# Attention and a mixture of experts on one core: the first expert's eight weight splits set 4 and 5 steps apart

## The chip, the core and the metric

The kernel runs on one core of a Trainium2 chip. A core has a matrix engine (PE, with its weight loads listed as PEld), a vector engine (DVE), a scalar engine (ACT), a general engine (POOL) and a sync engine (SP), which here only issues DMAs. Each runs its own instructions in the order in which they stand, and waits on semaphores for the others. The metric is the device time of one execution in microseconds.

## The reference: attention, then each token through one of eight experts

```python
# attention: q, k, v are (8, 8, 576, 64): batch, heads, sequence, head size
scores = (1 / np.sqrt(64)) * np.matmul(q, k.transpose(0, 1, 3, 2))
thresh = np.max(scores, axis=-1, keepdims=True) - tau
scores = np.where(scores >= thresh, scores, -1000000000.0)
scores = scores - np.max(scores, axis=-1, keepdims=True)
attn = np.exp(scores)
attn = attn / (np.sum(attn, axis=-1, keepdims=True) + 1e-09)
out = np.matmul(attn, v)
x = out.transpose(0, 2, 1, 3).reshape(4608, 512)
# experts: w_gate (512, 8), w1 (8, 512, 1024), w2 (8, 1024, 512)
logits = x @ w_gate
expert_idx = np.argmax(logits, axis=1)
probs = softmax(logits)                       # with 1e-09 in the denominator
gate_w = probs[np.arange(N), expert_idx]
for e in range(8):
    mask = expert_idx == e
    h = np.maximum(x[mask] @ w1[e], 0.0)
    out[mask] = gate_w[mask, None] * (h @ w2[e])
```

## The kernel before

**Arithmetic.** Every fp32 operand of a product is split into two fp16 tiles: a high part (the scaled value rounded) and a low part (what the rounding left). A product is then three fp16 matmuls. A weight split is `split_w`: one ACT instruction rounds a loaded piece `wf` (128 partitions by 1024) into the high half of `wb` (L817). For the first expert, and for it alone, the low part is made in two halves by `low_part`: PE copies the rounded half into PSUM with a matmul against the identity (`hi_w`, L254), and DVE subtracts it from the scaled weight (L255). The other experts' low parts are one DVE instruction each (L825).

**Attention.** The 64 heads are 32 pairs, numbered 0 to 31. A pair has 11 steps of scores `s` (for the row maxima, `nm`, on DVE) and 11 steps of transposed scores `st`. For each `st` tile ACT makes exponentials `e` (L423), DVE multiplies them with the threshold mask (L426), ACT rounds two tiles at a time into `ph` (L431) and POOL makes the low part `pl` (L432; for two tiles of the last pair DVE does it). PE then multiplies `ph` and `pl` with the values `vop` into `av` (L476). ACT copies `av` out (L486, L491). When a batch of four pairs is done, `finish` divides by the sums (`xn`, L537), splits the rows into `R` (L544 on ACT, L545 on POOL, or on DVE for the last batch), SP transposes them by DMA into `xTg` (L552), and PE makes the logits `lg` (L570). `route` and `ranks` find each token's expert and place; POOL sends the rows out to `xs` (L644), once ACT has written the gate weights into `R` (L637).

**Experts.** `fetch` gathers a block of 128 tokens of one expert from `xs` (into `Rm` or `spare`, L858) and transposes it (`xTm`, or within `spare`, L868). `gemm1` makes `h` (L913), `gemm2` makes `y` (L946). Blocks 0 to 3 belong to the first expert. Some of `gemm1` of block 0 stands among the last steps of attention.

**Order.** The program is written step by step: a step `k` holds one `st` and one `s` tile, and `plan` and `after` hang other work on a step, ahead of it, in the middle of it (MID) or behind it (END). Step 0 is the first `st` step of pair 0, and KEND = 352 is one past the last of pair 31. The `s` tiles of pair 31 are steps 320 to 330. From step 336 on expert work is mixed in, 0.15 pieces a step, and from 352 on a piece a step. A scheduler then lays out each engine's queue from this, so rows can change places against the written order. The first expert's work hangs at `k` = 312:

```python
for i in range(8):
    plan(k + WS0 + WSD * i, lambda i=i: split_w(*wseq[i]))          # WS0 = 6, WSD = 2
    if i + 2 < 8:
        plan(k + WS0 + WSD * i, lambda i=i: load_w(*wseq[i + 2]))
```

The first two loads are asked for at step 313 (`room`). There are two `wf` buffers, so the load of piece i + 2 can start when piece i's low part has been made. Loads, transposes and the three row DMAs of each pair (`CQ<-ptT`, L394) all stand in SP's one queue.

Of the kernel before, what the change touches and what calls it, by code (L numbers as in the profile page):

```python
# [39 lines left out]
SW = 64.0  # L40
# [10 lines left out]
def kernel(  # L51
# [119 lines left out]
    FRONT, MID, END = range(3)  # L171
# [3 lines left out]
    def plan(k, f, where=END):  # L175
        if urgent[0]:
            f = hurry(f)
        assert (k, where) >= (now[0], slot[0])
        acts.setdefault(k, ([], [], []))[where].append(f)

    def hurry(f):

        def g():
            was, urgent[0] = urgent[0], True
            with tc.high_priority():
                f()
            urgent[0] = was

        return g

    def after(k, f, where=END):
        plan(now[0] + k, f, where)
# [55 lines left out]
    def low_part(x, hi, lo, scale, nm):  # L248

        sc = ps_sc.tile([P, 512], F32, tag="sc", name=f"hi_{nm}")  # L250
        y = sc[:, 0:hi.shape[1]] if len(hi.shape) == 2 else (
            sc[:, 0:hi.shape[1] * hi.shape[2]].rearrange("p (t d) -> p t d", t=hi.shape[1])
        )
        nc.tensor.matmul(y, ident_h, hi, start=True, stop=True)  # L254
        nc.vector.scalar_tensor_tensor(lo, x, scale, y, ALU.mult, ALU.subtract)  # L255
# [541 lines left out]
    def load_w(e, w, c):  # L797

        i = int(e != 0)
        wq[e, w, c] = wf = pools[i].tile([P, F], F32, tag="wf", name=f"wf_{e}_{c}_{w}", bufs=2 + 6 * i)  # L800
        if e in range(E):
            load = nc.sync.dma_start(wf, w12[e, :, c, w])
            if e == 1:
                tc.keep_in_program_order(load)
            return
        if e not in regs:
            regs[e] = nc.sync.value_load(T["esi"][0:1, e - E:e - E + 1], min_val=0, max_val=E - 1)
        nc.sync.dma_start(wf, w12[ds(regs[e], 1), :, c, w].rearrange("o p f -> (o p) f"))
# [3 lines left out]
    def split_w(e, w, c):  # L812
        wf = wq.pop((e, w, c))

        o = (wb1, wb2)[w][0 if e == "x" else e % 2][:, c].rearrange("p (a h d) -> p a h d", a=w + 1, h=2)
        x = wf.rearrange("p (a d) -> p a d", a=w + 1)
        hi = nc.scalar.activation(o[:, :, 0], x, AF.Copy, scale=SW)  # L817
        if e == 0:
            tc.keep_in_program_order(hi)
            for i in range(2):  # L820
                t = slice(512 * i, 512 * i + 512)
                y = (x[:, i], o[:, i, 0], o[:, i, 1]) if w else (x[:, 0, t], o[:, 0, 0, t], o[:, 0, 1, t])
                after(2, lambda y=y, i=i: low_part(*y, SW, f"w{w}_{c}_{i}"), END if i else MID)
            return
        nc.vector.scalar_tensor_tensor(o[:, :, 1], x, SW, o[:, :, 0], ALU.mult, ALU.subtract)  # L825

# [58 lines left out]
    def chunks(g):  # L885

        return 8 * shape(g)[1] // P
# [105 lines left out]
    WS0, WSD = TUNE["ws0"], TUNE["wsd"]  # L993
# [9 lines left out]
    for n in range(NPAIR):  # L1003

        k = NSTEP * (n - 1) - LEAD - SL
# [5 lines left out]
    for g in range(NG):  # L1011
        k = 2 * NSTEP * g
# [80 lines left out]
    wseq = [(0, w, c) for w in range(2) for c in range(4)]  # L1093
    k = NSTEP * (NPAIR - 2) - LEAD - SL
    plan(k + 1, room)
    for i in range(8):
        plan(k + WS0 + WSD * i, lambda i=i: split_w(*wseq[i]))
        if i + 2 < 8:
            plan(k + WS0 + WSD * i, lambda i=i: load_w(*wseq[i + 2]))
    TABLES = {B - 3: tables0, B - 2: tables1, B - 1: tables2}  # L1100
    plan(KEND + 12, close)

# [10 lines left out]
    k = 0  # L1113
# [3 lines left out]
    for i, g in enumerate(groups):  # L1117
        for j, m in enumerate(g):
            if m >= NF + 2:
                k = max(at[i - 2] + TUNE["fa"] if i >= 8 else 0, at[i - 3] + chunks(groups[i - 3]) + 1)  # L1120
# [10 lines left out]
    for e in range(1, E + NL):  # L1131
        for w in range(2):
            for c in range(4):
                i = 4 * w + c
                if e == 1:
                    k = 64 + TUNE["w1a"] + TUNE["w1b"] * i
                elif e < E:
                    k = 64 * e + (TUNE["wa1"], TUNE["wa2"])[w] + 7 * i
                else:
                    k = 16 * NEARLY + 16 * PL // P * (e - E) + (TUNE["wl1"], TUNE["wl2"])[w] + 2 * c  # L1140
# [22 lines left out]
    def weights(j):  # L1163
        turn[0] = j + 1
        split_done.add(wseq[j])
        split_w(*wseq[j])
        if j + 8 < len(wseq):
            k, e = when[j][:2]
            moe(
                max(chunk[0] + 1, k - (14 if e == 2 else 24)) if e < E else chunk[0] + 1,  # L1170
                lambda: asked[0] == j, lambda: (asked.__setitem__(0, j + 1), load_w(*wseq[j + 8])),
            )
# [4 lines left out]
    if True:  # L1177
# [15 lines left out]
        k = first  # L1193
# [45 lines left out]
    with tc.For_i(NL, total) as m:  # L1239
        idx = small.tile([P, 2], I32, tag="idx", name="idx_x", bufs=1)  # L1240
        nc.vector.tensor_copy(idx.unsqueeze(1), T["row"][:, ds(m, 1)])
        bad = small.tile([P, 2], I32, tag="badx", name="bad_x", bufs=1)
        nc.vector.tensor_copy(bad.unsqueeze(1), T["bad"][:, ds(m, 1)])
        regs["x"] = nc.sync.value_load(T["esi"][0:1, ds(m, 1)], min_val=0, max_val=E - 1)
        for w in range(2):
            for c in range(4):
                load_w("x", w, c)
                split_w("x", w, c)
        slots["x"] = idx, bad, 0
        fetch("x")  # L1250
        for g in gemm1, gemm2:
            for _ in g(("x",)):
                chunk[0] += 1
            while mo:
                for _, f in mo.pop(min(mo)):
                    f()
# [52 lines left out]
```

## Time and profile before

| what | value |
|---|---|
| median of 3 runs | 975.57 us (975.03, 975.57, 981.8) |
| the profiled execution | 974.36 us, span 972.6 us |
| mean granted clock of TensorE | 0.993 |
| busy in the span | PE 932.8, DVE 696.2, ACT 652.7, POOL 559.0 us |
| instructions | 28577 |

The span runs from the first to the last instruction; the profiled execution is 1.76 us longer than its span. Busy time is an average over stages. The attention part fills the span to about 570 us, the experts the rest, and the change lies between 505 and 600 us.

### The profile page before, as it was taken

The numbers are of one execution on the slowest core, as the hardware profiler recorded it, in microseconds if no ns is written. First come the engines' busy times: TensorE is split into PE (matmuls) and PEld (weight loads), VectorE is DVE, ScalarE is ACT, GpSimd is POOL, SyncE is SP. The second block draws the span as 40 slices with busy tenths as digits, with TensorE's granted clock in tenths as the row PEclk, the third lists the DMA queues.
The fourth block names the chain that finished last, engine by engine and source line by source line (L and its number), as shares of the span: only waits on it lengthen the run. The fifth ranks groups of instructions, "written<-read, shape, count | busy, mean of one in ns | idle before, by whom it ended". The sixth has DMA issues, their size and how long they took to land. (4 is left out here: it accounts for less than half of the span.)

```text
span 972.6 us, 28577 instructions
## 1 busy us (share of the span) xinstructions
PE 932.8 (96%) x11548; PEld 604.0 (62%) x11548; DVE 696.2 (72%) x1413; ACT 652.7 (67%) x1111; POOL 559.0 (57%) x467
## 2 busy tenths in 40 slices
PE   7899999999999999999997989999999999999997
PEld 2355555556556556565664677776677666677684
DVE  8899999999989999999999756835243341432650
ACT  2789898998988998989889944435333342433651
POOL 6466887897977998869979851531221212221121
PEclk9899999999999999999999999999999999999999
DMA  7642555474654674654647569998475565656720
GB/s 202 185 135 73 142 137 143 93 196 123 130 161 134 162 147 134 176 146 104 154 133 207 95 168 304 396 234 212 127 231 157 166 177 155 206 143 209 219 103 28
DMA packets 142707, 159.19 MB, mean 164 GB/s; under 512 B 96361, under 2 KB 112747, under 8 KB 142572
## 3 DMA queue, kind: packets, MB, share of 16 engines
q1 hardware_dynamic: 125782, 100.03, 41.1%
q10 hardware_dynamic: 7638, 27.85, 9.2%
q0 software_dynamic: 9152, 29.45, 8.9%
q8 instruction: 92, 1.51, 0.7%
q14 instruction: 43, 0.35, 0.1%
HBM read 90.24 MB, written 19.44 MB: 113 GB/s over the span
## 5 line engine op out<-in xcount | busy, mean ns | idle before, releaser
L432 POOL TENSOR_TENSOR pl<-e,ph 128x1024 f16<-128x1024 f32 x158 | 335.8, 2136 | 90.0 <-ACT ph L431 50.8
L423 ACT ACTIVATE e<-st,ntau 128x512 f32<-128x512 f32 (+1 forms) x352 | 222.2, 651 | 49.0 <-PE st L407 34.8
L426 DVE SCALAR_TENSOR_TENSOR e<-st,e 128x512 f32<-128x512 f32 (+1 forms) x352 | 219.1, 635 | 8.4 <-ACT e L423 7.8
L913 PEld LDWEIGHTS <-wb 128*128 128x128 f16 x2304 | 189.4, 98 | 20.3 <-DMA xTm<-Rm 1.3
L946 PE MATMUL y<-wb,hl 128*128 128x512 f16 (+1 forms) x1056 | 201.6, 360 | 0.0
L370 DVE TENSOR_REDUCE nm<-s 128x1 f32<-128x512 f32 x300 | 188.2, 631 | 14.7 <-PE s L360 13.4
L913 PE MATMUL h<-xTm,wb 128*128 128x256 f16 (+2 forms) x2112 | 196.3, 254 | 0.9 <-DVE lg L609 0.9
L476 PE MATMUL av<-vop,ph 128*128 128x65 f16 (+3 forms) x3072 | 187.7, 195 | 2.0 <-ACT x L486 1.2
L476 PEld LDWEIGHTS <-ph 128*128 128x128 f16 (+1 forms) x3072 | 157.8, 100 | 46.5 <-issue 17.0
L431 ACT CAST ph<-e 128x1024 f16<-128x1024 f32 x160 | 166.5, 1041 | 5.1 <-DVE e L426 4.5
L476 PE MATMUL av<-vop,pl 128*128 128x65 f16 (+1 forms) x1536 | 167.1, 194 | 2.1 <-POOL pl L432 1.6
L476 PEld LDWEIGHTS <-pl 128*128 128x128 f16 (+1 forms) x1536 | 135.7, 100 | 33.5 <-issue 9.8
L946 PEld LDWEIGHTS <-hl 128*128 128x128 f16 (+1 forms) x1056 | 94.1, 100 | 97.8 <-issue 1.9
L407 PE MATMUL st<-CQ,ck 128*128 128x512 f16 (+3 forms) x640 | 136.4, 287 | 4.6 <-DMA CQ<-ptT 3.0
L825 DVE SCALAR_TENSOR_TENSOR wb<-wf,wb 128x1024 f16<-128x1024 f32 x88 | 104.1, 1220 | 50.1 <-ACT wb L817 48.6
L406 PE MATMUL st<-QK 128*128 128x512 f16 (+3 forms) x640 | 138.0, 293 | 0.4 <-DVE nm L370 0.2
L358 PE MATMUL s<-QK 128*128 128x512 f16 (+1 forms) x600 | 129.0, 292 | 0.4 <-DVE nm L370 0.2
L960 POOL DMA_INDIRECT out_dram<-o,gt x40 | 46.5, 1163 | 141.2 <-ACT o L957 125.6
L360 PE MATMUL s<-ck,CQ 128*128 128x512 f16 (+1 forms) x600 | 127.1, 287 | 0.5 <-DMA CQ<-hi 0.5
L901 ACT ACTIVATE hl<-h 128x512 f16<-128x512 f32 (+1 forms) x80 | 45.8, 573 | 108.3 <-PE h L913 108.3
L817 ACT ACTIVATE wb<-wf 128x1024 f16<-128x1024 f32 x96 | 97.7, 1050 | 27.2 <-DMA wf<-in_w_dram 11.3
L871 DVE COPY gt<-R 128x1 f32<-128x1 f32 x33 | 5.1, 153 | 121.4 <-DMA out_dram<-o,gt 109.4
(193 smaller groups left out, 1002.4 us busy)
## 6 DMA issues: line engine op xcount, KB each, us to landing
wf<-in_w_dram SPq DMA_DIRECT2D x96, 512.0 KB
qkf<-in_qk_dram ACTq DMA_DIRECT2D x29, 576.0 KB
vf<-in_v_dram ACTq DMA_DIRECT2D x15, 640.0 KB
QK<-hi SPq DMA_DIRECT2D x62, 144.0 KB
QK<-lo SPq DMA_DIRECT2D x62, 72.0 KB
QK<-hi SPq DMA_DIRECT2D x62, 72.0 KB
ck<-lo SPq DMA_DIRECT2D x62, 72.0 KB
CQ<-hi SPq DMA_DIRECT2D x62, 64.0 KB
```

The costliest lines, as they stand in the source:

```text
L358: nc.tensor.matmul(sc[rows, oc], d["QA"][a][:, cols], d["KB"][a][:, CH[c]], start=True, stop=False)
L360: nc.tensor.matmul(sc[rows, oc], d["CQ"][:, at:at + cols.stop - cols.start], d["CK"][a][:, CH[c]], start=False, stop=True,)
L370: nc.vector.tensor_reduce(o, sc[:, 0:width(t)], axis=AX.X, op=ALU.max, negate=True)
L406: nc.tensor.matmul(sc[rows, oc], d["KB"][a][:, cols], d["QA"][a][:, CH[c]], start=True, stop=False)
L407: nc.tensor.matmul(sc[rows, oc], d["CK"][a][:, cols], d["CQ"][:, q], start=False, stop=True)
L423: nc.scalar.activation(pf, sc, AF.Exp, bias=ntau, scale=0.125 / SS)
L426: nc.vector.scalar_tensor_tensor(pf, sc, 0.0, pf, ALU.is_ge, ALU.mult)
L431: nc.scalar.copy(h, pd)
L432: (nc.vector if (n, t) in PLV else nc.gpsimd).tensor_tensor(l, pd, h, ALU.subtract)
L476: nc.tensor.matmul(av[:, 0:D] if z == 2 else av, l if z == 1 else h, vop[:, tv, W:W + D] if z == 2 else vop[:, tv, 0:W], start=i in (0, NT ...
L913: nc.tensor.matmul(o, Wt[:, c, wh, f], x, start=c == 0 and z == 0, stop=c == 3 and z == 2,)
L946: nc.tensor.matmul(o, h[:, hh], Wt[:, f, wh, c], start=f == 0 and z == 0, stop=f == 7 and z == 2)
```

## The change

The eight splits of the first expert stood at steps 318, 320, 322 and so on to 332. They now stand at 318, 322, 326, 330 and then 336, 341, 346, 351. The load of piece i + 2 is asked for 4 steps behind split i, where it stood at the same step. The PE copies and DVE subtractions of a split stand 3 steps behind it, where they stood 2 behind. Nothing is added and nothing removed.

```diff
@@ split_w
             for i in range(2):
                 t = slice(512 * i, 512 * i + 512)
                 y = (x[:, i], o[:, i, 0], o[:, i, 1]) if w else (x[:, 0, t], o[:, 0, 0, t], o[:, 0, 1, t])
-                after(2, lambda y=y, i=i: low_part(*y, SW, f"w{w}_{c}_{i}"), END if i else MID)
+                after(3, lambda y=y, i=i: low_part(*y, SW, f"w{w}_{c}_{i}"), END if i else MID)
             return
@@
     for i in range(8):
-        plan(k + WS0 + WSD * i, lambda i=i: split_w(*wseq[i]))
+        z = k + (WS0 + 4 * i if i < 4 else WS0 + 18 + 5 * (i - 4))
+        plan(z, lambda i=i: split_w(*wseq[i]))
         if i + 2 < 8:
-            plan(k + WS0 + WSD * i, lambda i=i: load_w(*wseq[i + 2]))
+            plan(z + 4, lambda i=i: load_w(*wseq[i + 2]))
```

POOL's queue in pairs 29 and 30, before (`xn_2` to `xn_3` and their `R` are the second half of batch 6):

```order
L537 TENSOR_TENSOR xn_3_12178<-x_10432,rs_11882 128x512
L432 TENSOR_TENSOR pl_8_12004<-e_8_12002,ph_8_12003 128x1024
L432 TENSOR_TENSOR pl_4_12109<-e_4_12107,ph_4_12108 128x1024
L545 TENSOR_TENSOR R<-xn_2_12122,R 128x4x128
L545 TENSOR_TENSOR R<-xn_3_12178,R 128x4x128
L432 TENSOR_TENSOR pl_6_12204<-e_6_12202,ph_6_12203 128x1024
L432 TENSOR_TENSOR pl_0_12336<-e_0_12334,ph_0_12335 128x1024
L858 DMA Rm_12226<-xs,row_12176 128x514
```

The same place in POOL's queue with the change:

```order
L432 TENSOR_TENSOR pl_8_11993<-e_8_11991,ph_8_11992 128x1024
L537 TENSOR_TENSOR xn_3_12158<-x_10432,rs_11880 128x512
L432 TENSOR_TENSOR pl_4_12095<-e_4_12093,ph_4_12094 128x1024
L545 TENSOR_TENSOR R<-xn_2_12105,R 128x4x128
L432 TENSOR_TENSOR pl_6_12184<-e_6_12182,ph_6_12183 128x1024
L432 TENSOR_TENSOR pl_0_12313<-e_0_12311,ph_0_12312 128x1024
L545 TENSOR_TENSOR R<-xn_3_12158,R 128x4x128
L858 DMA Rm_12197<-xs,row_12156 128x514
```

The same instructions stand between the same neighbours; `R<-xn_3` has moved behind two `pl`.

ACT's queue near the end of pair 31, before (the last number of a name is a serial number; `e_6` and `ph_6` hold the `st` tiles 6 and 7, `ph_4` tiles 4 and 5; the `wb` splits are all done by here):

```order
L423 ACTIVATE e_4_12881<-st_5_12905,ntau 128x512
L431 CAST phc_10_12833<-e_10_12832 128x64
L637 ACTIVATE R<-sm_12572 128x4
L431 CAST ph_8_12791<-e_8_12790 128x1024
L423 ACTIVATE e_6_12942<-st_6_12939,ntau 128x512
L901 ACTIVATE hl_0_13061<-h_0_12726 128x512
L423 ACTIVATE e_6_12942<-st_7_12962,ntau 128x512
L431 CAST ph_4_12882<-e_4_12881 128x1024
L486 COPY x_12070<-av_1_12889 128x4x65
L491 COPY xh_10431<-av_1_12889 64x65 x2
L431 CAST ph_6_12943<-e_6_12942 128x1024
```

The same place in ACT's queue with the change:

```order
L423 ACTIVATE e_4_12868<-st_5_12892,ntau 128x512
L431 CAST phc_10_12819<-e_10_12818 128x64
L423 ACTIVATE e_6_12935<-st_6_12932,ntau 128x512
L431 CAST ph_8_12775<-e_8_12774 128x1024
L901 ACTIVATE hl_0_13061<-h_0_12704 128x512
L637 ACTIVATE R<-sm_12541 128x4
L423 ACTIVATE e_6_12935<-st_7_12955,ntau 128x512
L817 ACTIVATE wb_0_11670<-wf_3_1_12779 128x2x512
L486 COPY x_12050<-av_1_12876 128x4x65
L491 COPY xh_10431<-av_1_12876 64x65 x2
L431 CAST ph_4_12869<-e_4_12868 128x1024
```

The last weight split (`wb<-wf_3_1`) has moved in, `ph_4` stands behind it and behind the copies of `av`, and the gate weights (L637) stand behind `ph_8`, an exponential and `hl`. The cast of `ph_6` follows one small copy further on.

SP's queue after the end of attention, before (`spare` are blocks 3 and 4, `xTg_7` the transposed rows of the last batch, `xTm_5` block 5, `wf_1_...` pieces of the second expert):

```order
L802 DMA wf_1_0_0_13384<-in_w12_dram 128x1024
L868 DMA_TRANSPOSE spare_13231<-spare_13231 128x8x128 x2
L552 DMA_TRANSPOSE xTg_7_0_13426<-R_129 128x8x128 x2
L802 DMA wf_1_1_0_13441<-in_w12_dram 128x1024
L552 DMA_TRANSPOSE xTg_7_2_13445<-R_129 128x8x128 x2
L552 DMA_TRANSPOSE xTg_7_4_13456<-R_129 128x8x128
L802 DMA wf_1_2_0_13467<-in_w12_dram 128x1024
L802 DMA wf_1_3_0_13556<-in_w12_dram 128x1024
L868 DMA_TRANSPOSE xTm_5_13639<-Rm_5_13638 128x8x128
```

The same place in SP's queue with the change:

```order
L802 DMA wf_1_0_0_13384<-in_w12_dram 128x1024
L868 DMA_TRANSPOSE spare_13231<-spare_13231 128x8x128
L552 DMA_TRANSPOSE xTg_7_0_13426<-R_129 128x8x128 x2
L868 DMA_TRANSPOSE spare_13231<-spare_13231 128x8x128
L802 DMA wf_1_1_0_13441<-in_w12_dram 128x1024
L868 DMA_TRANSPOSE xTm_5_13639<-Rm_5_13638 128x8x128
L552 DMA_TRANSPOSE xTg_7_2_13445<-R_129 128x8x128 x2
L552 DMA_TRANSPOSE xTg_7_4_13456<-R_129 128x8x128
```

The first two transposes of the last batch stand one transpose earlier, the other three one transpose later.

## Rows read from the trace of the kernel before

**Rows 1.** Busy time by stretch: length, then PE, PEld, DVE, ACT, POOL; clock, DMA.
```profile
509.90:553.00 43.10, 35.66 (x572) 22.27 (x569) 36.40 (x87) 40.64 (x71) 40.85 (x33) 1.00 0.70 167
553.00:570.00 17.00, 17.00 (x413) 15.87 (x410) 11.00 (x29) 11.04 (x25) 11.02 (x9) 1.00 0.21 71
570.00:591.00 21.00, 17.98 (x225) 13.44 (x223) 11.77 (x23) 8.50 (x17) 6.42 (x9) 0.92 1.02 243
591.00:650.00 59.00, 58.91 (x662) 42.98 (x661) 37.58 (x98) 28.07 (x40) 26.25 (x26) 1.00 1.07 319
```
**Rows 2.** Who PE waited for, 500 to 600 us: total, times, longest (us).
```profile
PE hi_w L254 <- ACT wb L817: 4.0, 3, 1.5
PE lg L570 <- DMA xTg<-R: 3.0, 1, 3.0
PE hi_v L254 <- ACT vop L288: 1.1, 1, 1.1
```
**Rows 3.** POOL's groups, 509.9 to 553 us: busy, mean ns, idle before them.
```profile
L432 POOL TENSOR_TENSOR pl<-e,ph 128x1024 f16<-128x1024 f32 x12 | 25.5, 2135 | 1.7 <-issue 1.7
```
**Rows 4.** ACT's groups, 509.9 to 562 us.
```profile
L431 ACT CAST ph<-e 128x1024 f16<-128x1024 f32 x16 | 16.8, 1049 | 0.4 <-DVE e L426 0.4
L817 ACT ACTIVATE wb<-wf 128x1024 f16<-128x1024 f32 x8 | 8.4, 1051 | 0.0
```
**Rows 5.** What SP's queue waited for, 504 to 535 us: total, times, longest.
```profile
SPq L802 <- DVE wb L255: 13.2, 5, 3.8
```
**Rows 6.** POOL in order of time: start, duration, what [idle before, releaser].
```profile
548.60 4.24 POOL L432 TENSOR_TENSOR pl<-e,ph 128x1024 f16<-128x1024 f32 x2
...
554.80 2.14 POOL L432 TENSOR_TENSOR pl<-e,ph 128x1024 f16<-128x1024 f32 x1 [1.82 <-ACT sm L634]
...
557.37 1.01 POOL L644 DMA_INDIRECT xs<-R,posi  x1 [0.16 <-issue]
...
560.38 2.13 POOL L432 TENSOR_TENSOR pl<-e,ph 128x1024 f16<-128x1024 f32 x1 [0.56 <-ACT ph L431]
...
563.68 2.14 POOL L432 TENSOR_TENSOR pl<-e,ph 128x1024 f16<-128x1024 f32 x1
565.99 0.99 POOL L644 DMA_INDIRECT xs<-R,posi  x1 [0.17 <-issue]
569.78 0.98 POOL L858 DMA_INDIRECT spare<-xs,row  x1 [2.80 <-issue]
```
**Rows 7.** ACT in order of time.
```profile
556.53 0.24 ACT L637 ACTIVATE R<-sm 128x4 f32<-128x4 f32 x1
...
559.20 1.09 ACT L431 CAST ph<-e 128x1024 f16<-128x1024 f32 x1
...
561.04 1.04 ACT L431 CAST ph<-e 128x1024 f16<-128x1024 f32 x1
```
**Rows 8.** PE in order of time.
```profile
567.49 0.19 PE L476 MATMUL av<-vop,pl 128*128 128x65 f16 x1
...
581.91 0.46 PE L570 MATMUL lg<-wg,xTg 128*128 128x8 f16 x12 [3.02 <-DMA xTg<-R]
...
589.82 0.45 PE L570 MATMUL lg<-wg,xTg 128*128 128x8 f16 x12
```
**Rows 9.** SP's queue in order of time.
```profile
534.41 2.73 SPq L552 DMA_TRANSPOSE xTg<-R  x2
...
574.47 2.90 SPq L868 DMA_TRANSPOSE spare<-spare  x2
577.46 2.99 SPq L552 DMA_TRANSPOSE xTg<-R  x2
...
581.17 5.55 SPq L552 DMA_TRANSPOSE xTg<-R  x3
...
587.92 1.23 SPq L868 DMA_TRANSPOSE xTm<-Rm  x1
```
**Rows 10.** The four microseconds after PE's wait of 3 us, columns as in rows 1.
```profile
583.00:587.00 4.00, 4.00 (x64) 4.00 (x61) 1.98 (x3) 1.65 (x2) 0.47 (x1) 0.57 1.11 273
```

## The prediction

> **What bounds the kernel now.** I read the busy time by stretch first. From 591 us on PE is busy 58.91 of 59 us [rows 1], and nothing in the change adds or takes away work there, so the end of the program moves only by as much as PE's idle time ahead of 591 us changes. That idle time lies in two places. Between 509.9 and 553 us PE is busy 35.66 of 43.10 us, so 7.44 us are idle; between 553 and 570 us it is busy throughout; between 570 and 591 us it is idle 3.02 us [rows 1]. The list of waits names most of it: 4.0 us for `wb` splits ahead of the `hi_w` copies, 1.1 us for a `vop` split ahead of `hi_v`, and 3.0 us once for the transposes `xTg` of the last batch [rows 2].
>
> The question is whether the first two are a cause or only the place where the delay shows. In the same 43.1 us ACT is busy 40.64 us and POOL 40.85 us [rows 1]. POOL spends 25.5 us of that on twelve `pl` with 1.7 us of idle time in front of them, none of it put down to a missing cast [rows 3]. So POOL hardly ever waits for its inputs there, and PE cannot make `av` without `pl`. ACT has 16 casts `ph` (16.8 us) beside the eight weight splits (8.4 us) from 509.9 to 562 us [rows 4]. I conclude that POOL first, and ACT close behind, set the pace up to about 553 us, and that PE stands still somewhere whichever row the wait is written to. After 553 us PE is full and is waited for.
>
> **The change part by part.** All costs are against the profiled execution, 974.36 us; the median of the runs shown is 975.57, so 1.2 us are added at the end.
>
> *The eight splits, thinned out.* ACT does 8 x 1.05 = 8.4 us of them before and after [rows 4]; DVE's and PE's shares move with them. By the queue shown, ACT does the last one near the end of pair 31, where all eight were long done before. PE's 4.0 + 1.1 us of waits [rows 2] may therefore vanish as rows. What can be won by it is bounded by POOL: it has the same instructions up to `pl` of tiles 6 and 7 of pair 30, which end at 552.84 us (548.60 + 4.24) [rows 6]. Its idle time ahead of that is 43.10 - 40.85 = 2.25 us [rows 1], so at best everything behind comes 2.25 us earlier, at worst 0 or a little late. Most of that idle time stands in front of POOL's own DMAs and of `pl` with no releaser but "issue" [rows 3], so I take 0.5 us: **-0.5 us**, bounds -2.25 and 0.
>
> *A rule on this.* In 553 to 570 us ACT is busy 11.04 of 17 us, against 94% ahead of it [rows 1]. The Trainium skill (Perfetto Trace Analysis, Optimization Strategy) says that where the most contended engine changes between regimes, interleaving the regimes may improve performance; by it this change should pay, since it moves ACT work from the full regime into the lighter one. The sum by the rule would be a gain of the size of PE's named waits, which is a rival below. The trace agrees that the regimes differ but not, so far, that PE's waits are what is gained.
>
> *The loads, asked for later.* Before, SP's queue stood 13.2 us in five waits for the low parts that free a `wf` buffer [rows 5]; now a load is asked for a step after that. Behind it stand the row DMAs and the transposes, and PE's waits name neither of them in this stretch [rows 2], so what is taken away costs nothing now and brings nothing: **0**.
>
> *POOL's order in pairs 29 and 30.* `R<-xn_3` of batch 6 moves behind two `pl`, 2 x 2.14 = 4.3 us. Its transpose used to end its issue at 537.14 us with its neighbour (534.41 + 2.73) [rows 9]; now it comes up to 4.3 us later. That it lands late enough to hold PE is bounded by what PE has to do in the meantime, of which no row here gives the size; PE waited for no transpose of that batch [rows 2], so I take **0**, and as the upper bound +1, a quarter of the shift.
>
> *The tail of pair 31.* With the change the last `wb` split stands in ACT's queue ahead of `ph_4`, and so do the copies of `av`, which stood between `ph_4` and `ph_6`. The amount of ACT work ahead of `ph_6` is the same in both, so `ph_6` comes when it came, at 561.04 + 1.04 = 562.1 us [rows 7], if ACT idles as much as before. `ph_4` comes one cast ahead of it, at 561.1 and no longer at 560.3. POOL's `pl` of tiles 4 and 5 started at 560.38, having waited 0.56 us for just that cast [rows 6], and its sends and the last `pl` follow back to back; so this chain is 0.8 us later. PE does not feel it: the last `pl` ends at 565.82 [rows 6] and PE first uses it at 567.49 [rows 8], a slack of 1.67 us. The gate weights (L637, at 556.53 [rows 7]) stand behind a cast, an exponential and `hl` now, and the first send, at 557.37 [rows 6], moves by about half a microsecond, which POOL's 0.56 us of waiting takes in. What does feel it is the gather of blocks 3 and 4, which starts at 569.78 behind the last send (565.99 + 0.99) and its landing [rows 6]: **+0.8 us** on the start of SP's transposes at 574.47 [rows 9].
>
> *SP's order in the last batch.* The first pair of `xTg` stands one transpose earlier (2.90 / 2 = 1.45 us), the other three one later (1.23 us, that of `xTm`) [rows 9]. The first pair ended its issue at 577.46 + 2.99 = 580.45, and PE began its logits at 581.91 [rows 8], 1.46 us after. With 0.8 later and 1.45 earlier they begin at about 581.3. The other three ended their issue at 581.17 + 5.55 = 586.72 [rows 9], while the last logits came at 589.82 [rows 8], so 3.10 us after, with 1.64 us to spare over 1.46. They move by 0.8 + 1.23 = 2.03 us, that is 0.39 us more than the spare time: **+0.4 us** at the end of the last batch's logits.
>
> *The clock.* In the 4 us that follow 583 us the granted clock is 0.57 on average, in part the 1.2 GHz level, after PE stood idle for 3.02 us; 4 x 0.43 = 1.7 us of PE work are lost [rows 10]. A shorter wait may keep 2.4 GHz. But then PE meets the later transposes, and waits there. I take **0**, bounds -1.7 and +1.7.
>
> **The sum.** -0.5 + 0 + 0 + 0.4 + 0 = -0.1 us, of which the 0.8 us of the tail is already in the 0.4. That is 974.3 us on the profiled basis and 975.5 us against the median. The low bounds together are -2.25 - 1.7 = -3.95 us: 971.6. The high ones are the 1 us of batch 6, 2.03 us with no spare time, and 1.7 us of clock, 4.7 us: 980.3.
>
> **The rivals.** *PE's waits are real.* If POOL's idle time is not the limit (because casts that come sooner let it work without gaps behind 553 us, where it is busy 11.02 of 17 us [rows 1]), PE gets back 4.0 + 1.1 = 5.1 us [rows 2], and with a lost 1.2 GHz stretch up to 6.8: 970.5 to 968.8, say 970. For it speaks that PE is full from 553 on, so each microsecond PE gains early stays; against it that `av` needs `pl` and that the last `pl` leaves only 1.67 us of room. As a mechanism: ACT has 6 us free behind 553 us [rows 1] and the splits go there. The rule quoted above from the Trainium skill (Perfetto Trace Analysis, Optimization Strategy) expects this one.
>
> *ACT pays in the tail.* Four splits, 4 x 1.05 = 4.2 us [rows 4], now lie in pairs 30 and 31 and shortly before, on the chain cast, `pl`, send, gather, transposes. If ACT cannot use the time that it gains earlier, since it then waits for PE's `st` and `av`, each of these casts delays the chain. The sends and the gather then come up to 4.2 us later, the last transposes 4.2 + 1.23 = 5.4 us, less the 1.64 us to spare: +3.8 us, 979.4. It decides from the point at which ACT's idle time ahead of `ph_6` grows by more than the 1.6 us to spare.
>
> *The queues hardly change.* That would be the forecast's time as well; the queues shown say that they do.
>
> **How the numbers follow.** A measurement of this kernel tells about 1%, 10 us, from no change. I give the forecast 0.6, the first rival 0.2, the second 0.18, and 0.02 to something larger. Predicted is 975.5 us. For eight in ten the range takes in the forecast's bounds and most of both rivals: 970 to 979.5. A gain of over 1% would take all of the 7.44 + 3.02 us that PE is idle, so 0.02. Over 1% slower needs more than twice the second rival, 0.03. The rest, 0.95, is within 1%.
>
> **What would show it.** Right: POOL still busy about 95% up to 553 us, its last `pl` of pair 30 ending within 1 us of 552.8 and the last one of pair 31 near 566.5; PE's waits on `hi_w` smaller, with others (`pl`, `ph`, `st`) in their place; the first logits of the last batch a little earlier, the last ones at about the same time. The first rival would show the last `pl` of pair 31 by 563 us and PE's idle time up to 553 us at 3 us or less. The second would show ACT waiting for PE between 540 and 560 us and the gather of block 3 starting at 572 us or later. I am wrong altogether if PE is idle behind 591 us, since then a weight load or a gather of the experts has become late.

## The result, and the profile after

The change makes the kernel slower. In the first round the changed kernel took 986.1 us (median of 6 runs, 984.04 to 987.46) and the kernel before 975.3 (6 runs, 973.68 to 981.8), a ratio of 1.0085 with a 95% interval of 1.0061 to 1.0108. Two later rounds gave 1.0115 [1.0087, 1.0144] and 1.0112 [1.0097, 1.0128]. Predicted were 975.5 us and a range up to 979.5. In another round the 19 runs of before itself fall into two groups, four at 982 to 984 us and fifteen at 990 to 997, so that a ratio to its median says little there.

The profiled execution took 986.42 us with a span of 984.7, against 974.36 and 972.6, so 12.06 us more. The first view is the busy time by stretch after the change; columns are the length, then PE, PEld, DVE, ACT, POOL, the granted clock, the DMA share and GB/s, as in [rows 1].

```profile
509.90:553.00 43.10, 33.31 (x465) 19.93 (x463) 29.87 (x71) 32.82 (x59) 37.14 (x29) 0.84 0.64 134
553.00:570.00 17.00, 14.29 (x280) 11.15 (x278) 13.89 (x29) 15.08 (x28) 8.18 (x8) 1.00 0.38 107
570.00:591.00 21.00, 20.35 (x372) 17.19 (x368) 12.81 (x33) 9.34 (x21) 12.10 (x12) 1.00 0.66 153
591.00:650.00 59.00, 54.53 (x640) 39.38 (x639) 34.78 (x97) 24.53 (x35) 18.71 (x22) 0.97 1.05 324
536.00:542.60 6.60, 6.60 (x88) 4.40 (x89) 3.35 (x7) 4.68 (x8) 6.11 (x6) 0.50 0.66 130
546.50:553.00 6.50, 4.95 (x65) 3.09 (x66) 3.50 (x12) 3.15 (x7) 2.23 (x3) 0.50 0.87 130
```

PE is now idle 9.79 + 2.71 + 0.65 + 4.47 = 17.6 us in these four stretches, against 7.44 + 0 + 3.02 + 0.09 = 10.6 in [rows 1]: 7.0 us more. The clock takes as much again. Before, it fell short of full speed by 21 x 0.08 = 1.7 us; now by 43.1 x 0.16 + 59 x 0.03 = 8.7 us, and the last two rows show where: two stretches of 6.5 us at half the clock, which is the 1.2 GHz level. Idle time that falls within such a stretch is counted in both sums (in the last row 1.55 us, worth 0.8 at half the clock), which is a part of why 14 us stand against 12.06 measured.

Next, who PE waited for from 500 to 610 us: total, times, longest wait in us. It answers to [rows 2].

```profile
PE lg L570 <- DMA xTg<-R: 9.5, 4, 4.4
PE hi_w L254 <- ACT wb L817: 3.2, 3, 2.7
PE pst L381 <- DVE row L669: 1.4, 1, 1.4
PE hi_v L254 <- ACT vop L288: 1.3, 1, 1.3
```

The longest wait is new: 4.4 us for a transpose of batch 6. The rows around it, from the timelines of POOL, SP, DVE, PE and ACT (start, duration, what, idle time before and its releaser):

```profile
538.14 1.16 POOL L545 TENSOR_TENSOR R<-xn,R 128x512 f16<-128x512 f32 x1
539.46 1.01 POOL L858 DMA_INDIRECT Rm<-xs,row  x1 [0.16 <-issue]
540.78 0.96 POOL L858 DMA_INDIRECT Rm<-xs,row  x1 [0.30 <-issue]
...
537.78 0.41 SPq L802 DMA_DIRECT2D wf<-in_w_dram  x1
539.33 1.26 SPq L552 DMA_TRANSPOSE xTg<-R  x1
...
548.04 0.15 DVE L871 COPY gt<-Rm 128x1 f32<-128x1 f32 x1 [4.31 <-DMA Rm<-xs,row]
...
548.05 0.48 PE L570 MATMUL lg<-wg,xTg 128*128 128x8 f16 x12 [4.40 <-DMA xTg<-R]
...
549.45 0.69 ACT L423 ACTIVATE e<-st,ntau 128x512 f32<-128x512 f32 x1 [5.99 <-PE st L407]
```

`R<-xn_3` ends at 539.30, and its transpose is issued beside it. Within 3 us there are now a 512 KB load of a weight piece, this transpose and two gathers. The transpose's issue ends at 540.59 and PE gets the data at 548.05, 7.5 us later. Before, the pair's issue ended at 537.14 (534.41 + 2.73 in [rows 9]), ahead of both gathers, and PE did not wait:

```profile
533.24 2.27 POOL L545 TENSOR_TENSOR R<-xn,R 128x512 f16<-128x512 f32 x2
...
539.85 1.01 POOL L858 DMA_INDIRECT Rm<-xs,row  x1 [0.16 <-PE hi_w L254]
541.17 0.96 POOL L858 DMA_INDIRECT Rm<-xs,row  x1 [0.30 <-issue]
...
541.75 1.35 PE L570 MATMUL lg<-wg,xTg 128*128 128x8 f16 x48
```

With the change PE, DVE and ACT all stand still in the meantime, since `lg` stands in PE's queue ahead of the next `st`, and the copy `gt<-Rm` in DVE's ahead of the next mask. What moved through the DMA engines in this time, and how long a gather took (median us from issue to landing, 538 to 548.5 us):

```profile
541.00:548.00 7.00, 2.66 (x34) 1.69 (x31) 1.38 (x2) 2.46 (x4) 5.20 (x4) 0.74 0.99 110
Rm<-xs,row POOLq DMA_INDIRECT x2, 8.1
```

The engines are 99% busy and move 110 GB/s. From there the delay runs on to the tail of attention and the last batch:

```profile
566.60 0.21 ACT L637 ACTIVATE R<-sm 128x4 f32<-128x4 f32 x1
567.26 1.06 ACT L817 ACTIVATE wb<-wf 128x1024 f16<-128x1024 f32 x1
...
567.09 1.26 POOL L644 DMA_INDIRECT xs<-R,posi  x1 [2.66 <-ACT R L637]
...
573.49 2.14 POOL L432 TENSOR_TENSOR pl<-e,ph 128x1024 f16<-128x1024 f32 x1
...
579.52 0.98 POOL L858 DMA_INDIRECT spare<-xs,row  x1 [2.75 <-DVE hl L902]
...
568.38 0.59 PE L254 MATMUL hi_w<-wb,ident_h 128*128 128x512 f16 x2 [2.71 <-ACT wb L817]
...
597.39 0.48 PE L570 MATMUL lg<-wg,xTg 128*128 128x8 f16 x12 [3.90 <-DMA xTg<-R]
```

The gate weights are written at 566.60 (556.53 in [rows 7]), so the first send waits for them; the last `pl` starts at 573.49 (563.68) and the gather of block 3 at 579.52 (569.78, both [rows 6]): 10 us later each. PE waits 2.71 us for the last weight split, which now lies in pair 31.

### The profile page after: what moved, and what is told of

Read it like the earlier page. It is cut to its first block, busy times and chain, and to the rows that moved or that the text cites. A ratio compares the mean times of both kernels' runs of the same rounds, so it can differ in the third digit from the quotient of the medians.

```text
span 984.7 us, 28577 instructions
## 1 busy us (share of the span) xinstructions
PE 937.3 (95%) x11548; PEld 605.8 (62%) x11548; DVE 696.2 (71%) x1413; ACT 652.7 (66%) x1111; POOL 556.1 (56%) x467
## 5 line engine op out<-in xcount | busy, mean ns | idle before, releaser
L913 PEld LDWEIGHTS <-wb 128*128 128x128 f16 x2304 | 189.0, 98 | 19.6 <-DMA xTm<-Rm 0.5
L476 PE MATMUL av<-vop,ph 128*128 128x65 f16 (+3 forms) x3072 | 190.7, 195 | 1.5 <-ACT x L486 1.2
L476 PEld LDWEIGHTS <-ph 128*128 128x128 f16 (+1 forms) x3072 | 159.8, 100 | 47.2 <-issue 18.5
L476 PE MATMUL av<-vop,pl 128*128 128x65 f16 (+1 forms) x1536 | 169.4, 194 | 2.5 <-POOL pl L432 1.9
```

The source lines that it names most:

```text
L476: nc.tensor.matmul(av[:, 0:D] if z == 2 else av, l if z == 1 else h, vop[:, tv, W:W + D] if z == 2 else vop[:, tv, 0:W], start=i in (0, NT ...
L913: nc.tensor.matmul(o, Wt[:, c, wh, f], x, start=c == 0 and z == 0, stop=c == 3 and z == 2,)
```

## The experiments

Three theories. **J** (jam): the late low part of batch 6 sends its transpose out beside a load and two gathers. **A** (ACT in the tail): the late splits delay casts, sends and the gather. **L**: the order of SP's transposes in the last batch. The runs were made in four rounds, and rounds differ: before took about 976 us in two of them, 991.5 (median of 19 runs, 982 to 997) and 984.6 (median of 25, 980 to 1001) in the others. The record has one chip number for the 991.5 us round and for one of the 976 us rounds, so what makes them differ is open. Ratios to before in the same round are compared, and those of the last two rounds tell little. The table has each kernel's ratio, PE's wait for batch 6's last transpose with the time from the end of its issue to the first of the logits that need it, and the start of the gather of block 3 after POOL's first send of batch 5 (a point ahead of the change), in us. Where PE didn't wait, the time to the logits is only an upper bound of the landing. Each kernel has one profile per round. In the diffs `no` is a dependency that fixes an order and no wait, and lines that only keep an instruction for it are left out.

```
kernel             ratio   95% interval     wait  issue end to lg  gather
before             1                        0     5.5              59.5
change_again       1.0115  [1.0087, 1.0144] 3.2   6.3              70.2
change_third       1.0112  [1.0097, 1.0128] 2.7   6.1              67.7
r_early_third      1.0043  [1.0022, 1.0063] 0.7   1.9              62.0
load_behind_again  1.0060  [1.0046, 1.0074] 3.3   3.5              66.3
gather_behind      1.0066  [1.0046, 1.0086] 1.2   2.5              63.3
split_late4        1.0048  [1.0032, 1.0064] 0.5   3.3              62.0
tail_early         1.0083  [1.0053, 1.0113] 0.3   3.0              66.1
last_pinned        1.0099  [1.0075, 1.0123] 4.2   7.3              69.0
in the 991.5 us round:
lag3_only          0.9891  [0.9859, 0.9923] 0.8   4.3              62.6
spacing_only       1.0005  [0.9974, 1.0036] 0     3.2              65.9
load_behind        1.0023  [0.9974, 1.0072] 1.0   4.0              65.9
r_early            0.9908  [0.9872, 0.9944] 0.8   2.0              63.8
in the 984.6 us round:
r_early_again      1.0041  [0.9990, 1.0093] 0.7   1.9              62.1
late4_last         1.0117  [1.0049, 1.0186] 0     3.9              61.2
lag3_again         0.9998  [0.9942, 1.0053] 1.2   4.3              63.2
last4_by3          1.0052  [0.9998, 1.0105] 0     5.1              64.4
```

### Parts of the change alone

**lag3_only** and **lag3_again**: before, with the low parts 3 steps behind.

```diff
-                after(2, lambda y=y, i=i: low_part(*y, SW, f"w{w}_{c}_{i}"), END if i else MID)
+                after(3, lambda y=y, i=i: low_part(*y, SW, f"w{w}_{c}_{i}"), END if i else MID)
```

> The splits stand 2 steps apart as before; only their low parts stand 3 steps behind. In the queues both last transposes of batch 6 stand together again behind all the weight loads. Theory J (the last transpose of batch 6 met a weight load and two gathers in the DMA queues, and PE stood still behind it, 4.4 us and then at 1.2 GHz): PE's wait for that transpose under 1 us, time within 3 us of before (972 to 978 us). Theory A (weight splits in ACT's queue during pairs 30 and 31 delay the casts): the splits are all done before pair 31, so within 3 us of before too. Theory L (the transposes of the last batch stand behind others in SP's queue): here five of the order's changes are other ones, the first pair of that batch is early, so 1 to 3 us faster than before.

> Before with the low parts 3 steps behind the splits in place of 2, a second time (the first, on a chip where before took 991 us, gave 0.9891). POOL keeps both low parts of batch 6 ahead of the pl's and no split moves into the tail, so by J and A the ratio is 0.998 to 1.003; that this edit is a gain of its own would give 0.989 to 0.995.

The 0.9891 of the first did not come back: 0.9998 [0.9942, 1.0053]. All four runs of the first (981.9 to 983.6 us) lie where the four quickest of before lay in that round. The 3 steps are neither the loss nor a gain that these runs can tell.

**spacing_only**: the new spacing with low parts 2 steps behind and loads at the split.

```diff
-                after(3, lambda y=y, i=i: low_part(*y, SW, f"w{w}_{c}_{i}"), END if i else MID)
+                after(2, lambda y=y, i=i: low_part(*y, SW, f"w{w}_{c}_{i}"), END if i else MID)
-            plan(z + 4, lambda i=i: load_w(*wseq[i + 2]))
+            plan(z, lambda i=i: load_w(*wseq[i + 2]))
```

> The splits stand 4 and 5 steps apart as in the change, the low parts 2 steps behind as before (where the loads are asked for does not alter the queues here). The low part of the last rows of batch 6 stands behind one pl instead of two, a weight load just ahead of its transpose. Theory J: the transpose starts about 2 us sooner than with the change but still meets the load and the gathers, a wait of 2 to 4 us; 3 to 9 us slower than before. Theory A: the splits stand in pairs 30 and 31 as with the change, so 6 to 10 us slower than before, with waits on casts.

The ratio says little in this round, and the expected wait of 2 to 4 us did not come. The trace says more: the low part is as late as in the change (538.85 us) and the gathers follow it, but the load that the expectation had there is not issued beside it, and the transpose reaches PE within 3.2 us of the end of its issue.

```profile
538.85 1.15 POOL L545 TENSOR_TENSOR R<-xn,R 128x512 f16<-128x512 f32 x1
...
541.24 1.25 SPq L552 DMA_TRANSPOSE xTg<-R  x1
...
545.64 0.46 PE L570 MATMUL lg<-wg,xTg 128*128 128x8 f16 x12
```

Being late beside the gathers does not jam, then. The gather still comes at 65.9 us here; what makes it late in this kernel was not tried.

### The jam: r_early, load_behind, gather_behind

**r_early**, **r_early_again**, **r_early_third**: the changed kernel with batch 6's last division and low part pinned ahead of three `pl` (an order only, no wait).

```diff
+            if (n, t) == (NPAIR - 3, REST):
+                tc.add_manual_dep(pl.ins, kept["xn"].name, no, reason="order")
+            if (n, t) == (NPAIR - 3, 7):
+                tc.add_manual_dep(ph.ins, kept["high"].name, no, reason="order")
+                tc.add_manual_dep(pl.ins, kept["low"].name, no, reason="order")
```

> The change, with the division, rounding and subtraction of the last rows of batch 6 held ahead of the two pl that the change put in front of them (as before), so that both last transposes of that batch start together, ahead of the load and the gathers. Theory J: both land before 541 us, no wait of PE for them over 0.5 us, 4 to 8 us faster than the change. Theory A: no gain over 2 us, since the splits stay in pairs 30 and 31.

> The kernel of r_early a second time, beside a before that runs near 975 us: the changed kernel with only batch 6's last rows (xn_3 and its low part) ahead of the pl's on POOL. The changed kernel's ratio to before was 1.0115. Theory J (the late low part sends its transpose out beside the gathers and the sixth load): the wait of 3.2 to 4.4 us for batch 6's transposes and the half clock around it go, and the ratio is 1.004 to 1.007, what is left being the tail (split_late4 had 1.0048). If the tail alone makes the loss and J is only where it shows: 1.009 to 1.012.

> As r_early, for the first time beside the changed kernel on one chip. Theory J: the late low part costs 5 to 7 us of the change's 11, so this kernel's time is 0.5 to 0.7% under the changed one's and about 0.5% over that of before (what the tail costs, by split_late4). Rival (the wait only shows what the tail and the last batch cost anyway): within 0.3% of the changed kernel.

**load_behind**, **load_behind_again**: the load of piece 5 behind the last transpose of batch 6 on SP.

```diff
+            if (e, w, c) == (0, 1, 1):
+                tc.add_manual_dep(load.ins, kept["turn"].name, no, reason="behind the transpose")
```

> The change, with one weight load (the sixth piece) put behind the last transpose of batch 6 in SP's queue; ACT's and POOL's queues stay as with the change. Theory J with the load to blame: the transpose lands within 3 us of its issue, PE's wait for it 1 us or less, 4 to 8 us faster than the change. Theory J with the gathers to blame: the wait stays at 3 us or more and the time within 2 us of the change. Theory A: within 1.5 us of the change, since no cast moves.

> The changed kernel with the load of piece 5 (of 0 to 7) behind batch 6's last transpose on SP; POOL's order as in the change. If the load's data in the way makes the transpose late, it lands within 4 us of the end of its issue (the changed kernel: 7.5 us, spacing_only, which has no load there: 3.1) and PE waits under 1.5 us for it; the time is 0.2 to 0.4% under the changed kernel's. If the two gathers do it, it lands as late as in the changed kernel and the time is the same within 0.1%.

**gather_behind**: the gathers of blocks 0 and 1 behind one more `pl`.

```diff
-            after(1 + m, lambda m=m: fetch(m))
+            after(9 + m, lambda m=m: fetch(m))
+            if m == 0:
+                tc.add_manual_dep(get, kept["pl"].name, no, reason="order")
```

> The changed kernel with the two gathers of blocks 0 and 1 behind one more pl on POOL (2.1 us later); the load stays where it is. If the gathers make the transpose late, it lands within 5 us of the end of its issue and PE's wait for it falls under 2 us; if the load does, it still lands 6 us or more after it and PE waits 3 us or more.

In one round the changed kernel (change_third) took 987.9 us, r_early_third 979.9, load_behind_again 982.6 and gather_behind 982.6 (medians), before 976.8. The four timelines, the changed kernel first:

```profile
541.13 1.26 SPq L552 DMA_TRANSPOSE xTg<-R  x1
...
548.51 0.46 PE L570 MATMUL lg<-wg,xTg 128*128 128x8 f16 x12 [2.71 <-DMA xTg<-R]
```

r_early_third:

```profile
536.72 3.27 SPq L562 DMA_TRANSPOSE xTg<-R  x2
541.68 0.45 SPq L812 DMA_DIRECT2D wf<-in_w_dram  x1
...
541.89 0.46 PE L580 MATMUL lg<-wg,xTg 128*128 128x8 f16 x12 [0.67 <-DMA xTg<-R]
```

load_behind_again:

```profile
539.72 1.26 SPq L552 DMA_TRANSPOSE xTg<-R  x1
541.08 0.53 SPq L804 DMA_DIRECT2D wf<-in_w_dram  x1
...
544.47 0.48 PE L572 MATMUL lg<-wg,xTg 128*128 128x8 f16 x12 [3.26 <-DMA xTg<-R]
```

gather_behind:

```profile
539.87 1.26 SPq L554 DMA_TRANSPOSE xTg<-R  x1
...
542.10 1.01 POOL L861 DMA_INDIRECT Rm<-xs,row  x1 [0.16 <-DVE e L426]
...
543.66 0.46 PE L572 MATMUL lg<-wg,xTg 128*128 128x8 f16 x12 [1.16 <-DMA xTg<-R]
```

All three parties are needed for the jam. With the load moved by one transpose or the gathers by one `pl`, the transpose lands 3.5 and 2.5 us after its issue in place of 6.1, and either edit gives back 5.3 us. J expected one culprit; both are. The wait of 3.26 us in load_behind_again is as long as in the change, so that expectation (under 1.5) fell: PE came to its logits early there and stood at 541.2 already. The time went down by 0.5% where 0.2 to 0.4 was expected. With the low part early, 8.0 of the 11.1 us are gone, where 5 to 7 were expected; r_early and r_early_again show the same waits of 0.7 to 0.8 us, in rounds whose ratios can't be used for this. The three edits are not equally clean. In load_behind_again POOL's and ACT's rows keep the changed kernel's order up to 580 us, so its 5.3 us are put down to the jam. In gather_behind and r_early_third the scheduler also lays out rows of the tail anew (the gate weights stand earlier on ACT, in r_early_third the first send on POOL too, and PE's wait for the last split is 0.38 there in place of 2.71 us), so not all of their 5.3 and 8.0 us is the transpose.

### The tail: split_late4, tail_early

**split_late4**: before, with the last four splits at the change's steps.

```diff
-        plan(k + WS0 + WSD * i, lambda i=i: split_w(*wseq[i]))
+        z = k + (WS0 + WSD * i if i < 4 else (336, 341, 346, 351)[i - 4] - 312)
+        plan(z, lambda i=i: split_w(*wseq[i]))
```

> The kernel before with only the last four splits moved to the changed kernel's steps 336, 341, 346 and 351; loads, low parts and the first four splits stay as before, and so does POOL's order of batch 6 (both low parts ahead of pl of tiles 6). Theory A: these four casts sit in ACT's queue among those of pairs 30 and 31, and the gather of block 3 comes 63 to 65 us after the first send of batch 5 in place of 59.5; the ratio to before is 1.003 to 1.006. Theory J: batch 6's transposes come as before, PE's wait for them is under 1 us, and without the jam the gather comes by 61 us; the ratio is within 0.2% of 1.

It takes 980.8 us against 975.85, ratio 1.0048: the ratio of theory A, at 5 us. PE waits for the last split and again for the last batch:

```profile
560.48 0.59 PE L254 MATMUL hi_w<-wb,ident_h 128*128 128x512 f16 x2 [1.86 <-ACT wb L817]
...
578.40 1.72 SPq L868 DMA_TRANSPOSE xTm<-Rm  x1
580.22 6.28 SPq L552 DMA_TRANSPOSE xTg<-R  x3
...
586.62 0.48 PE L570 MATMUL lg<-wg,xTg 128*128 128x8 f16 x12 [5.14 <-DMA xTg<-R]
```

The gather comes 62.0 us after the first send, 2.4 later than in before: between the two theories' numbers. The other part of the loss lies behind the gather. The last batch's first logits start 15.4 us after it, in before 12.1, and block 5's transpose now stands ahead of that batch's on SP. So the four late splits and the order that came with them cost 5 us together; this run does not part A from L.

**tail_early**: r_early with the last four splits 2 steps apart, ahead of pair 31's casts.

```diff
-        z = k + (WS0 + 4 * i if i < 4 else WS0 + 18 + 5 * (i - 4))
+        z = k + WS0 + (0, 4, 8, 12, 14, 16, 18, 20)[i]
...
-            plan(z + 4, lambda i=i: load_w(*wseq[i + 2]))
+            plan(z + (4 if i < 3 else 0), lambda i=i: load_w(*wseq[i + 2]))
```

> The changed kernel with batch 6's low part ahead of the pl's (as in r_early) and with the last four splits 2 steps apart, at 330 to 338 in place of 336 to 351. r_early had the gather of block 3 at 63.8 us after the first send of batch 5, the changed kernel 69.6, before 59.5. Theory A: with the splits out of the tail the gather comes at 59.5 to 61 us and the ratio to before is 0.998 to 1.003. Without A (what is left in r_early comes from elsewhere) the gather stays at 63 to 65 us and the ratio is 1.003 to 1.006.

It gave 1.0083, where r_early_third gave 1.0043 (the intervals overlap a little), and it has a wait that the expectation did not have. ACT's and PE's waits, 505 to 575 us, and two of ACT's splits:

```profile
ACT wb L828 <- DMA wf<-in_w_dram: 5.3, 3, 2.9
...
PE hi_w L254 <- ACT wb L828: 6.5, 5, 2.5
...
543.28 1.06 ACT L828 ACTIVATE wb<-wf 128x1024 f16<-128x1024 f32 x1 [1.95 <-DMA wf<-in_w_dram]
...
547.61 1.06 ACT L828 ACTIVATE wb<-wf 128x1024 f16<-128x1024 f32 x1 [2.89 <-DMA wf<-in_w_dram]
```

With two `wf` buffers, thin first splits make the later loads late, and splits close behind each other then wait for them, with the casts of attention queued behind on ACT. So this kernel doesn't test A; it shows what thinning out the first four splits alone brings in here.

### The last batch: last_pinned, late4_last

**last_pinned** is the changed kernel, **late4_last** is split_late4, each with the last batch's transposes on SP as before.

```diff
+                if b == B - 1:
+                    tc.add_manual_dep(t.ins, kept[4].name, no, reason="order")
+            if m == 5:
+                tc.add_manual_dep(t.ins, kept[B - 1, 4].name, no, reason="order")
```

> The changed kernel with the last batch's transposes on SP in the order of before: all five of batch 7 behind both of blocks 3 and 4 and ahead of block 5's. Theory L: the last logits come 2 to 2.5 us earlier after the gather of block 3 (before 20.5 us, changed 23.0), and the time is 0.2 to 0.3% under that of the changed kernel. Rival: the logits wait for data that the gather and the loads hold up, in whatever order; then the interval stays 22.5 us or more and the time equals that of the changed kernel within 0.1%.

> split_late4 (before with the last four splits at 336 to 351) with the last batch's five transposes pinned ahead of block 5's on SP, as in before. split_late4 had PE wait 5.14 us for the first of these transposes, at 586.62 us; in before it was 3.02 us at 581.91. Theory L (SP's order): the transposes are issued 1.7 us earlier, the first logits come by 585 us, and the ratio to before falls from 1.0048 to 1.002 to 1.003. Theory A (the gather of blocks 3 and 4 and what ACT owes set it): the ratio stays at 1.004 to 1.006.

last_pinned takes 986.26 us beside change_again's 986.77. Its last logits come earlier (598.77 us; 602.85 in change_again), but PE then waits at the next step of the chain:

```profile
591.41 0.46 PE L573 MATMUL lg<-wg,xTg 128*128 128x8 f16 x12 [3.23 <-DMA xTg<-R]
...
607.60 0.19 PE L624 MATMUL rk<-oh,before 128*128 128x8 f16 x1 [2.67 <-DVE run L616]
```

The last logits come 19.6 us after the gather of block 3, 22.9 in change_again and 20.0 in before, so SP's order does set that interval, as L says. The time moved by 0.5 us, where L expected 2 to 3; four runs of each, spread over 4.1 and 3.5 us, do not exclude L's number, but the wait at `rk` shows where the gain went. late4_last's first logits came without the wait of 5.14 us, but its `rk` waited 2.67 us, and all four runs (993.0 to 998.4) lie in the upper part of what before gave in that round (980 to 1001): inconclusive.

### A milder form: last4_by3

The first four splits 2 apart as before, the last four 3 apart.

```diff
-        plan(k + WS0 + WSD * i, lambda i=i: split_w(*wseq[i]))
+        z = k + (318, 320, 322, 324, 327, 330, 333, 336)[i] - 312
+        plan(z, lambda i=i: split_w(*wseq[i]))
...
-            plan(k + WS0 + WSD * i, lambda i=i: load_w(*wseq[i + 2]))
+            plan(z + 0, lambda i=i: load_w(*wseq[i + 2]))
```

> A mild form of the change: the first four splits 2 steps apart as before, the last four 3 apart (327, 330, 333, 336), loads and low parts as before. POOL's order in batch 6 is that of before, and ACT has the last split ahead of ph_8 of pair 30. By J and A nothing is lost: ratio 0.998 to 1.002; if thinning out the splits gives PE back its waits for wb (4.0 us in before), 0.996 to 0.998. SP's queue in the last batch has the transposes xTg_7_0 between the two of blocks 3 and 4; should that order cost what L says, 1.002 to 1.004.

1.0052 [0.9998, 1.0105]: no gain that these runs can tell, and perhaps a loss. Its profile has PE waiting up to 1.57 us for `wb` still, and 1.14 us for `ph` (0.5 before). No kernel here is shown to beat the one before.

## Why the prediction was wrong

**The step that failed** is the one on POOL's order in pairs 29 and 30. It took 0, at most +1, for `R<-xn_3` moving behind two `pl`, because PE had waited for no transpose of that batch. The shift was read right (3.8 us: it ended at 539.30, before at 533.24 + 2.27 = 535.51), but it was priced at a quarter of the shift at most, and nothing in the working lets the transpose take longer to land. At its new time it met a load and two gathers, and PE got it 7.5 us after the end of its issue. Undoing that order gave 8.0 of the 11.1 us back, with some rows of the tail; moving the load or the gathers aside gave 5.3 each. The gather stands in the very next row of POOL's queue as shown, and the prediction did not ask what the transpose would now share the DMA engines with.

**The loads, asked for later, were put at 0.** SP's queue waits 4.6 us for the low parts from 504 to 535 us, in place of 13.2, and no run parts out whether that is worth anything. But the sixth load now falls into the jam, which load_behind_again shows at 5.3 us. It is the same error from SP's side.

**The clock was put at 0**, within 1.7 either way. In the profile it costs 8.7 us against 1.7 before. The first of the two stretches at 0.50 comes after PE's waits of 1.42 us for `row` and 1.35 for `vop`, the second begins within its wait of 4.40. r_early_third still has such stretches, but loses 6 x 0.28 twice there, 3.4 us, up to 553 us. From 509.9 to 650 us the clock takes 8.5 us in change_third, 8.5 in load_behind_again and 5.1 in r_early_third. So load_behind_again got its 5.3 us back without the clock, and up to 3.4 of r_early_third's 8.0 us may have come by it; how much the clock alone costs was not separated.

**The tail** is the second term that failed. The forecast had +0.8 us on the gather, absorbed to +0.4, on the condition that ACT idles as much as before. It idled more: 43.10 - 32.82 = 10.3 us up to 553 us, 6.0 of it in the jam, where before had 2.5; split_late4, which has no jam, has 5.5. The gate weights were put half a microsecond later, though the cast ahead of them alone takes 1.05 us [rows 4]; POOL's first send waited 2.66 us for them. The second rival (four casts on the chain, the gather up to 4.2 us later, 979.4 us) came near: split_late4 costs 5.0 us, 2.4 of it on the gather, and what r_early_third leaves is 3.1. Both of its signs came in the change, ACT waiting for PE between 540 and 560 us (5.99 us at 549.45) and the gather behind 572, but there the jam makes the wait. In split_late4 ACT's idle time grows by 3.0 us, more than the 1.6 that the rival named as the turning point, but between 538 and 562 us ACT waits 2.2 us for DVE's mask and 0.3 for `st`, so that it waits for PE, as the rival has it, is not shown. The forecast priced the last split alone, which stands ahead of `ph_4` in the order shown, and not the other three.

**SP's order in the last batch** (+0.4) was mis-sized for the logits: the last ones come 22.6 us after the gather's start, in before 20.0, and pinning the order back brought them from 22.9 to 19.6. For the time it was small as far as these runs tell, since PE then waits at `rk`.

**The splits, thinned out** (-0.5, and the first rival's 5.1): PE's waits for `wb` went down from 4.0 to 0.5 in the stretch to 553 us and came back as 2.7 in the tail, with `pst`, `vop` and the transpose in their place, as "PE stands still somewhere" had it. The rule from the Trainium skill (Perfetto Trace Analysis, Optimization Strategy) that interleaving regimes may improve performance did not pay here: ACT's work went where ACT had room, but PE and the sends waited for it there.

**Wrong altogether** was to be known by PE idle behind 591 us; it is idle 4.47 us there, though by the last batch's transposes and not by a load of the experts.

## What to carry to other kernels

When a DMA that someone waits for moves by a few microseconds, list what else will be on the DMA engines at its new time, from every queue; the old landing time holds only for the old neighbours. A wait that vanishes from PE's list is no gain until the engine behind it is shown to be ahead. And thin-out edits under a scheduler should be read for what else they reorder: here a subtraction that went behind two instructions on POOL cost more (5.3 to 8.0 us) than the waits that the edit was read to win back (5.1).

## What was unexpected of the hardware

- In one round batch 6's last transpose landed 1.9 to 3.5 us after the end of its issue when the load or the gathers were out of its way, and 6.1 us with both (7.5 in the first round). The gathers took 6.8 us with both (8.1 in the first round) and 4.6 in gather_behind. The Trainium skill (DMA: Bandwidth & Descriptors, Queues, rings and completion order) says that each DMA engine takes turns between the queue rows that it has work for, a packet at a time; the trace agrees as far as transfers from SP's and POOL's queues all became late together at a DMA share of 0.99, while no run here shows the turns.
- PE's waits of 1.42 and 1.35 us, which ended at 533.29 and 535.33, were followed by 6.6 us at the 1.2 GHz level (0.50 granted). In before, waits of 1.37 and 1.14 us that ended at 535.00 and 537.68 were not; the clock stayed at 1.00. What makes the difference was not tried. The two waits with the change, then the two before:

```profile
533.29 0.28 PE L381 MATMUL pst<-ident,r 128*9 128x128 f32 x1 [1.42 <-DVE row L669]
535.33 0.30 PE L254 MATMUL hi_v<-vop,ident_h 128*128 128x320 f16 x1 [1.35 <-ACT vop L288]
...
535.00 0.59 PE L254 MATMUL hi_w<-wb,ident_h 128*128 128x512 f16 x2 [1.37 <-ACT wb L817]
537.68 0.44 PE L254 MATMUL hi_v<-vop,ident_h 128*128 128x320 f16 x2 [1.14 <-ACT vop L288]
```

- In the two rounds where before took 985 and 991 us PE stands still in most kernels between matmuls of `gemm1` with nothing to wait for that the profile shows, in load_behind 4.3 us from 600 to 650 us; the same kernel has no such row there in load_behind_again.

```profile
PE h L918 <- issue: 4.3, 9, 1.2
```
